# Reordered first loads, one chunk's statistics on ScalarE, and moved filler products in an attention and gated-MLP kernel

## The chip, the cores and the metric

The kernel runs on one core of one Trainium2 chip. The metric is device time in microseconds (us). Nine runs of the kernel before the change have a median of 799.55 us (799.35 to 801.16).

## The reference

Two residual blocks follow each other on x of shape 2048 x 1024, in bf16.

```python
h  = x + A(layernorm(x), wq, wk, wv, wo, beta)
h2 = h + B(layernorm(h), w_in, w_sp, b_sp, w_out)
```

A is attention with 32 heads of width 32 over four segments of 512 rows. Within a segment it is causal softmax attention. Beside it each head keeps a memory M and a sum z of earlier segments: with phi(t) = t + 1 for t > 0 and exp(t) otherwise, the memory's output is phi(q) M / (phi(q) z + 1e-6), and after each segment M gains phi(k)^T v and z gains the sum of phi(k). Both outputs are mixed by the gate sigmoid(beta) of the head, and the result is multiplied by wo.

B is a gated MLP: z = gelu(x w_in) with 3584 columns is split in halves z1 and z2, z2 is layer-normalized and mixed along the sequence by the 2048 x 2048 matrix w_sp, plus a bias b_sp for each row; the product with z1 goes through w_out.

## The kernel before, in words

The whole program is a list of operations. Each call of `G.op` (L93) records an operation with its engine, a cost in ns and the tiles that it reads and writes, from which its dependences follow. `schedule` (L150) then plays the list through a model of five engines: TensorE (PE) keeps the order in which its operations were recorded; ScalarE (ACT), VectorE (DVE), GpSimd (POOL) and SyncE (SP) take whatever is ready, by the place in the list plus a priority. The model's costs, with its model of DMA time (L211 to L215), thus fix the order on these four engines once and for all; on the chip each engine runs its own order and waits on semaphores (`link`, L232; `run`, L318). SP issues all DMAs, and at the end waits for the last count of every DMA semaphore (L1041, `dma_ends` of L304).

The start (L507 to L786). PE runs 14 warm-up products on zeros (`N_WARM`). SP loads x chunk by chunk (128 rows each; chunk 0 in two halves of its columns), wv, wq and wk by halves of their columns (`w_half`), and beta. `layernorm` (L524) of a chunk is two `bn_stats` of 512 columns and a `bn_aggr` on VectorE, the addition of epsilon (`pts1`) and the power -0.5 (`ptt`) on GpSimd, and the scaling (`ts`) in place on VectorE. `x_turn_pe` (L567) turns a chunk with 8 transposes on PE, four to a bank of PSUM; the first four are copied to XNT by VectorE, the others by ScalarE. Of the products with wv's first half, 8 to a chunk, the turn of the next chunk is put ahead of number 5 (`AT`). Then come the first q and k products and beta's gate.

The attention (L789 to L883) goes through 32 groups n of four heads (segment s = n // 8, c = n % 8) in 16 pairs. A pair has five logit rounds. In each, PE makes logits in four banks (`logits`, 4 or 8 products with 32 rows), ScalarE takes the exponential of all 2048 columns into E, and GpSimd masks it; the next round's logits need those banks again. Between the rounds stand other products in an order written out by hand: the projections `Pq` and `Pk`, the products with V (`X`, `MZU`, which ends in `combine` on VectorE and a transposing DMA into OT), and five slots of filler products. A filler is a V group (`v_group`: 8 products of 512 columns, copied by ScalarE) of a later or the same segment, or a wo group (`wo_group`: 8 products, an addition on VectorE, and at its second half the output's store, the layernorm of h and a transposing DMA). `plan` lays out which fillers go to which n, `order` to which slots: (2, 4, 0, 4, 1) in pairs 0 to 14, with two fillers in pairs 0 to 3, 12 and 14 and four in the others. In segment 0, `Pq` of n > 0 is copied by VectorE, otherwise by ScalarE. `chores` records the loads and layernorms of later chunks, and the second halves of wq, wk and wo.

The gated MLP (L886 to L1015) follows with products of 512 columns, gelu on ScalarE and additions and multiplications on VectorE. The change doesn't touch it.

Of the kernel before, what the change touches and what calls it, by code (L numbers as in the profile page):

```python
# [10 lines left out]
ACTF = mybir.ActivationFunctionType  # L11
# [24 lines left out]
class _Prog:  # L36
# [113 lines left out]
    def schedule(self):  # L150
        ops = self.ops
        n = len(ops)
        for o in ops:
            o.users = []
            o.ndep = len(o.deps)
            o.t0 = o.t1 = None
        for o in ops:
            for d in o.deps:
                ops[d].users.append(o.idx)
        pe_seq = [o.idx for o in ops if o.eng == PE]  # L160
        pe_at = 0
# [12 lines left out]

        while done < n:
            best = None
            if pe_at < len(pe_seq):
                o = ops[pe_seq[pe_at]]
                if o.ndep == 0:
                    best = (max(free[PE], rt[o.idx]), 0, PE, o.idx)  # L180
            for e in (ACT, DVE, POOL, SP):
                r, a = ready[e], avail[e]
                while r and r[0][0] <= free[e]:
                    _, p, i = heapq.heappop(r)
                    heapq.heappush(a, (p, i))
# [24 lines left out]
            free[e] = start + cost  # L210
            if o.dma:  # L211
                b = max(start + 2000.0, dma_free)
                dma_free = b + o.nbytes / 370.0
                o.t1 = dma_free + 50.0
                free[e] = start + cost  # L215
            else:
                o.t1 = start + cost + o.lag
            order[e].append(i)
            done += 1
            for u in o.users:  # L220
                w = ops[u]
                w.ndep -= 1
                t = o.t1 + (lag_same if w.eng == e and not o.dma else lag_x)
                if t > rt[u]:
                    rt[u] = t
                if w.ndep == 0 and w.eng != PE:
                    heapq.heappush(ready[w.eng], (rt[u], w.prio, u))
        self.order = order
        return max(o.t1 for o in ops)


    def link(self):  # L232
# [66 lines left out]
        for i in self.order[SP] + self.order[POOL] + self.order[ACT]:  # L299
            o = ops[i]  # L300
            if o.dma:
                cnt[o.sem] += 16
                o.semval = cnt[o.sem]
        self.dma_ends = [(dsem[j], cnt[j]) for j in range(npool)]  # L304
        for o in ops:
            w = []
            for q, v in o.waits.items():
# [22 lines left out]
def bass_sequential_preLN__memory_aug_infini_attn__mixer_gmlp__prompt_kernel(  # L330
# [87 lines left out]

    N_WARM = 14
    AT = [5, 5, 5, 9]  # L420
    BYACT = [0, 0, 0, 0]
    PS = nc.alloc_psum_tensor("ps", [128, 8, 512], F32)
    G.psum = PS.name

# [9 lines left out]
    def mm(o, lhsT, rhs, start, stop):  # L434
        n = n_of(rhs)
        G.op(PE, lambda e: e.matmul(o, lhsT, rhs, start=start, stop=stop), [lhsT, rhs], [o],  # L436
             max(n / 2.4 + 2.6, 25.0), lag=166, name="mm " + lhsT.tensor.name + " " + rhs.tensor.name)
# [50 lines left out]
    def pset(o, v):  # L488
        G.op(POOL, lambda e: e.memset(o, v), [], [o], (150 + n_of(o)) / 1.2, name="memset")

    def dma(o, i, transpose=False, after=False):
        nb = n_of(o) * list(o.ap)[0][1] * mybir.dt.size(o.dtype)
        d = G.op(SP, lambda e: e.dma_start(o, i, transpose=transpose), [i], [o], 1230.0 if transpose else 400.0, dma=True,  # L493
             nbytes=nb * (2.1 if transpose else 1.0), name=("T:" if transpose else "D:") + o.tensor.name)
        if after:
            d.deps.add(G.last_pe)
# [11 lines left out]
    G.op(DVE, lambda e: e.memset(ZERO[:], 0.0), [], [ZERO[:]], 200, name="memset")  # L508
    for k in range(N_WARM):
        mm(PS[:, 7, :], ZERO[:, 0:128], ZERO[:], True, True)  # L510
    for h in range(2):
        dma(XIN[0][:, h * 512:(h + 1) * 512], x2d[0:128, h * 512:(h + 1) * 512])
    iot = tens("iot", [128, 128], I32, R_E)
    G.op(POOL, lambda e: e.iota(iot[:], [[1, 128]], base=0, channel_multiplier=-1), [], [iot[:]], 400)
    pset(MHALF[:], -0.5)
# [5 lines left out]

    ln_rr = [0]

    def layernorm(src, dst, w, prio=0, by_act=False):  # L524
        late[0] = prio
        k = ln_rr[0] % 4
        ln_rr[0] += 1
        nch = (w + 511) // 512
        cs = w // nch
        for ci in range(nch):  # L530
            si, so = src[:, ci * cs:(ci + 1) * cs], STATS[k][:, ci, :]
            G.op(DVE, lambda e, si=si, so=so: e.bn_stats(so, si), [si], [so], (cs + 143) / 0.96, name="bn_stats",  # L532
                 prio=late[0])
        sa, mv = STATS[k][:, 0:nch, :], MV[k][:, 0:2]
        G.op(DVE, lambda e: e.bn_aggr(mv, sa), [sa], [mv], 250, name="bn_aggr", prio=late[0])  # L535
        pts1(RS[k][:], MV[k][:, 1:2], LN_EPS, ALU.add)
        ptt(RS[k][:], RS[k][:], MHALF[:], ALU.pow)
        if by_act:
            nm, mean, rs = MV[k][:, 2:3], MV[k][:, 0:1], RS[k][:]
            G.op(POOL, lambda e: e.scalar_tensor_tensor(nm, mean, -1.0, rs, ALU.mult, ALU.mult), [mean, rs], [nm],  # L540
                 220, name="nmr")
            act(dst, src, ACTF.Identity, scale=rs, bias=nm)
        else:
            ts(dst, src, MV[k][:, 0:1], RS[k][:], ALU.subtract, ALU.mult)
        late[0] = 0


    NJ = [512, 384, 256, 128]
# [13 lines left out]
    def x_load(tc):  # L562
        dma(XIN[tc % 4][:], x2d[tc * 128:(tc + 1) * 128, :])
# [4 lines left out]
    def x_turn_pe(tc):  # L568
        dst = XNT[0][:, :, tc * 128:(tc + 1) * 128]
        for h in range(2):  # L570
            bb = bank().bitcast(BF16)
            for i in range(4):
                c = 4 * h + i
                tr(bb[:, i * 128:(i + 1) * 128], XIN[tc][:, c * 128:(c + 1) * 128])
            bv = bb[:, 0:512].rearrange("p (c n) -> p c n", c=4)
            if h == 0:
                late[0] = -200
                copy(dst[:, 0:4, :], bv)
                late[0] = 0
            else:  # L580
                act(dst[:, 4:8, :], bv, ACTF.Copy)

    def x_turn(tc):
        s, tcl = divmod(tc, 4)
# [158 lines left out]
            dma(HNT[s][:, :, tcl * 128:(tcl + 1) * 128], hx[:], transpose=True)  # L743


    x_load(1)
    w_half(WV, A_wv, 0)
    x_load(2)
    x_load(3)
    w_half(WQ, A_wq, 0)  # L750
    w_half(WK, A_wk, 0)
# [2 lines left out]
    for i in range(2):  # L754
        pset(V[i][:, :, :, 32:34], 1.0)
    bank_rr[0] = 0
    for tcl in range(4):
        layernorm(XIN[tcl][:], XIN[tcl][:], D, by_act=BYACT[tcl])
    x_turn_pe(0)
    for tcl in range(4):  # L760
        b = bank()
# [25 lines left out]


    bank_set[0] = [4, 5, 6, 7]  # L789
    plan = []  # L790
    for n in range(32):
        s, c = divmod(n, 8)
        vs, wos = [], []
        if s == 0:
            vs = [(0, c, 1)] if c < 4 else [(1, c - 4, 0)]
        elif s <= 2:
            vs = [(s, 2 * c, 1), (s, 2 * c + 1, 1)] if c < 2 else [(s + 1, c - 4, 0)] if c >= 4 else []
        elif c < 4:
            vs = [(3, c, 1)]
        if 1 <= s <= 3:  # L800
            k = (0, 0, 2, 2, 1, 1, 1, 1) if s <= 2 else (0, 0, 1, 1, 1, 1, 2, 2)
            wos = [(s - 1, g) for g in range(sum(k[:c]), sum(k[:c + 1]))]
        plan.append((vs, wos))
    WINB = []
    for k, (c0, w) in enumerate(((1792, 512), (2304, 512), (2816, 512), (3328, 256), (0, 512), (512, 512),
                                 (1024, 512), (1536, 256))):
# [33 lines left out]

    for pair in range(16):
        a, b = 2 * pair, 2 * pair + 1
        fill = [(v_group, x) for n in (a, b) for x in plan[n][0]] + [(wo_group, x) for n in (a, b) for x in plan[n][1]]
        for n in (b + 1, b + 2):
            if n < 32:
                for x in plan[n][1]:
                    if x[1] % 2 == 0:
                        h_load(4 * x[0] + x[1] // 2)
        slots = [[] for _ in range(5)]
        order = (2, 4, 0, 4, 1) if pair < 15 else (2, 2, 3, 4)  # L850
        for k, x in enumerate(fill):
            slots[order[k]].append(x)

# [217 lines left out]
```

## Time and profile before

| | |
|---|---|
| median of 9 runs | 799.55 us |
| the profiled execution's own time | 800.15 us |
| its span in the trace | 798.4 us |
| PE, VectorE, ScalarE, GpSimd busy | 791.7, 369.8, 293.0, 140.2 us |
| first transpose of x on PE | 7.54 us |
| first q product | 18.58 us |
| first logits of pair 0, of pair 1 | 22.15, 36.82 us |
| last logits of the attention | 294.15 us |
| last addition on VectorE | 795.69 us |

Lines of the profile read thus. In a timeline: start, length, engine, line, operation, tiles (out<-in), shape, count, and in brackets how long the engine stood idle ahead of it and for whom. In a list of waits: who waited for whom, the total in us, how often, the longest. In a table of stretches: the stretch and its length, then busy us and number of instructions for PE, PE's weight loads, VectorE, ScalarE and GpSimd, the granted clock, the share of the DMA engines and GB/s. The line of an operation is often that of a helper: L436 is `mm`, L441 the logits, L445 the transposes, L450 `act`, L466 the scaling, L532 `bn_stats`, L493 every DMA, L1042 the final waits.

### The profile page before, as it was taken

What the parts mean: (1) busy time and instruction counts of PE and PEld (TensorE: products, weight loads), DVE (VectorE), ACT (ScalarE), POOL (GpSimd) and SP (SyncE); (2) the same over time, 40 slices, a digit from 0 to 9 for tenths busy, and PEclk for the clock granted to TensorE, in tenths of its full rate; (3) what the DMA queues carried; (4) which work ended last, traced back from release to release, by engine and by line L of the source; (5) the groups of instructions that cost most, each with busy time, mean ns of one, the idle gap of its engine ahead of it and who ended that gap; (6) DMA issues with size and microseconds to landing.
All of it is one profiled execution on the core that took longest, in us unless ns stands there. A gap on an engine that the chain in (4) does not pass through costs nothing.

```text
span 798.4 us, 12667 instructions
## 1 busy us (share of the span) xinstructions
PE 791.7 (99%) x5380; PEld 382.0 (48%) x5380; DVE 369.8 (46%) x849; ACT 293.0 (37%) x329; POOL 140.2 (18%) x273
## 2 busy tenths in 40 slices
PE   8999999999999999999999999999999999999998
PEld 3455555555554555445445454444444444444444
DVE  5883578968875586704224051133223223322332
ACT  2888867776788872133333333100000000000000
POOL 2464434443443341100001010000000000000000
PEclk9999999999999999999999999999999999999999
DMA  9757514452433548520000026803400620021001
GB/s 298 157 140 162 130 41 99 94 101 69 77 71 89 171 90 227 169 46 1 0 1 1 16 54 133 200 1 71 120 27 1 137 81 1 0 60 53 1 7 47
DMA packets 128457, 64.80 MB, mean 81 GB/s; under 512 B 95504, under 2 KB 120336, under 8 KB 128400
## 3 DMA queue, kind: packets, MB, share of 16 engines
q1 hardware_dynamic: 128400, 63.99, 33.2%
q8 instruction: 42, 0.69, 0.4%
q14 instruction: 15, 0.12, 0.1%
HBM read 32.51 MB, written 8.39 MB: 51 GB/s over the span
## 4 chain that ended last, share of the span: by engine, by line
PE 97%; DMA 1%; ACT 1%; DVE 1%; SPq 0%; issue 0%
PE ps L436 94%; PE ps L441 3%; DMA xin<-in_A_x_dram 1%; ACT e L450 0%; DVE stats L532 0%; SPq L493 0%; PE ps L445 0%; ACT qk L450 0%; DVE xin L466 0%; ACT ex L450 0%; DVE xnT L462 0%; DVE hx L472 0%; DVE mv L535 0%
## 5 line engine op out<-in xcount | busy, mean ns | idle before, releaser
L436 PE MATMUL ps<-wspT,z 128*128 128x512 bf16 x896 | 194.0, 379 | 0.0
L450 ACT ACTIVATE e<-ps 128x2048 bf16<-128x2048 f32 x80 | 149.7, 1872 | 40.0 <-PE ps L441 40.0
L436 PEld LDWEIGHTS ps<-wspT,z 128*128 128x128 bf16 x896 | 87.5, 98 | 105.8
L450 ACT ACTIVATE z<-ps 128x512 bf16<-128x512 f32 x120 | 68.2, 568 | 140.2 <-PE ps L436 140.2
L472 DVE TENSOR_TENSOR tg<-ps,brow 128x512 bf16<-128x512 f32 x56 | 38.7, 691 | 152.7 <-PE ps L436 122.5
L436 PE MATMUL ps<-win,hnT 128*128 128x512 bf16 (+1 forms) x512 | 97.8, 353 | 0.0
L436 PE MATMUL ps<-wout,y 128*128 128x512 bf16 (+2 forms) x462 | 97.4, 373 | 0.0
L436 PE MATMUL ps<-hnT,win 128*128 128x512 bf16 x448 | 97.3, 379 | 0.0
L653 POOL TENSOR_SCALAR_AFFINE_SELECT e<-e 128x1024 bf16<-128x1024 bf16 (+1 forms) x80 | 75.7, 946 | 107.0 <-ACT e L450 106.6
L532 DVE BATCH_NORM_STATS2 stats<-z 128x6 f32<-128x448 bf16 x64 | 39.9, 623 | 94.1 <-ACT z L450 92.6
L472 DVE TENSOR_TENSOR hx<-hx,ps 128x512 bf16<-128x512 bf16 (+1 forms) x65 | 43.7, 678 | 84.6 <-PE ps L436 82.3
L436 PEld LDWEIGHTS ps<-win,hnT 128*128 128x128 bf16 x512 | 50.0, 98 | 47.9
L436 PEld LDWEIGHTS ps<-wout,y 128*128 128x128 bf16 x462 | 44.6, 98 | 52.4
L436 PEld LDWEIGHTS ps<-hnT,win 128*128 128x128 bf16 x448 | 43.8, 98 | 52.3
L436 PE MATMUL ps<-wv,xnT 128*128 128x512 bf16 x256 | 60.2, 379 | 0.9 <-DMA wv<-in_A_wv_dram 0.9
L436 PE MATMUL ps<-xnT,wk 128*128 128x512 bf16 (+2 forms) x264 | 60.8, 374 | 0.0
L436 PE MATMUL ps<-xnT,wq 128*128 128x512 bf16 x256 | 60.8, 381 | 0.0
L436 PE MATMUL ps<-wo,oT 128*128 128x512 bf16 x256 | 59.0, 379 | 0.0
L486 POOL TENSOR_SCALAR rs<-mv 128x1 f32<-128x1 f32 x48 | 11.1, 230 | 193.1 <-DVE mv L535 191.7
L436 PEld LDWEIGHTS ps<-v,e 128*128 128x128 bf16 x1280 | 40.1, 96 | 9.1 <-issue 0.9
L436 PE MATMUL ps<-v,e 128*128 128x33 bf16 x1280 | 42.1, 178 | 0.0
L436 PEld LDWEIGHTS ps<-wo,oT 128*128 128x128 bf16 x256 | 24.7, 98 | 28.5 <-DVE ta L472 0.2
(58 smaller groups left out, 573.1 us busy)
## 6 DMA issues: line engine op xcount, KB each, us to landing
win<-in_B_w_in_dram SPq DMA_DIRECT2D x6, 1024.0 KB, 6.1
hx<-in_A_x_dram SPq DMA_DIRECT2D x16, 256.0 KB, 2.9
out_dram<-hx SPq DMA_DIRECT2D x16, 256.0 KB, 2.4
hx<-out_dram SPq DMA_DIRECT2D x16, 256.0 KB, 2.7
out_dram<-hx SPq DMA_DIRECT2D x31, 128.0 KB, 1.8
xin<-in_A_x_dram SPq DMA_DIRECT2D x15, 256.0 KB, 3.9
wout<-in_B_w_out_dram SPq DMA_DIRECT2D x2, 1792.0 KB, 10.0
wv<-in_A_wv_dram SPq DMA_DIRECT2D x2, 1024.0 KB, 9.6
```

Of the source, the lines that this page charges most:

```text
L436: G.op(PE, lambda e: e.matmul(o, lhsT, rhs, start=start, stop=stop), [lhsT, rhs], [o], max(n / 2.4 + 2.6, 25.0), lag=166, name="mm " + lhs ...
L441: G.op(PE, lambda e: e.matmul(o, lhsT, rhs, start=True, stop=True, tile_position=(32 * i, 0)), [lhsT, rhs], [o], n / 2.4 if last else 3.5, ...
L450: G.op(ACT, lambda e: e.activation(o, i, func, scale=scale, **kw), r, [o], ((172 if inps(i) else 224) + n_of(i)) / 1.2 + 26, prio=prio, na ...
L472: G.op(DVE, lambda e: e.tensor_tensor(o, a, b, op), [a, b], [o], vcost(o, [a, b], fast), name="tt", prio=late[0])
L486: G.op(POOL, lambda e: e.tensor_single_scalar(o, i, s, op), [i], [o], 220 if n_of(o) < 8 else 220 + 2.5 * n_of(o), name="pts1", prio=late[0])
L532: G.op(DVE, lambda e, si=si, so=so: e.bn_stats(so, si), [si], [so], (cs + 143) / 0.96, name="bn_stats", prio=late[0])
L653: G.op(POOL, lambda e: e.affine_select(d, d, pat, ALU.is_ge, 0.0, base=0, channel_multiplier=-1), [d], [d], 1270 if j else 640, name="mask")
```

## The change

Six edits go together. The planner's model of DMA time gets other constants, with 700 ns for transfers of 200,000 bytes or more, and the planned cost of `bn_aggr` goes from 250 to 210. The final waits are sorted by the planned end of each semaphore's last transfer. The first loads are recorded in the order x0 (two halves), x1, x2, wv in three pieces of its rows, x3, wq, wk. Chunk 1's mean and sum of squares come from two ScalarE passes with accumulator outputs (`layernorm_act`); for the other three chunks epsilon is added on VectorE, and the second `bn_stats` of a chunk is recorded as depending on the scaling of the chunk before it that VectorE treats. The copies of the turned chunks are assigned by the table `TCOPY`: both to VectorE for chunk 0. And the fillers of each pair, their slots and the engine that copies a V group are written out in `FILL`: pair 0 has four V groups instead of two, pair 4 two instead of four, and the pairs behind it have between two and five.

```diff
             if o.dma:
-                b = max(start + 2000.0, dma_free)
-                dma_free = b + o.nbytes / 370.0
-                o.t1 = dma_free + 50.0
+                b = max(start + 1850.0, dma_free)
+                dma_free = b + o.nbytes / 350.0
+                o.t1 = dma_free + (700.0 if o.nbytes >= 200000 else 50.0)
...
-        self.dma_ends = [(dsem[j], cnt[j]) for j in range(npool)]
+        ends = {}
+        for o in ops:
+            if o.dma and o.semval == cnt[o.sem]:
+                ends[o.sem] = o.t1
+        self.dma_ends = [(dsem[j], cnt[j]) for j in sorted(range(npool), key=lambda j: ends[j])]
...
-    BYACT = [0, 0, 0, 0]
+    TCOPY = [(DVE, DVE), (DVE, ACT), (DVE, ACT), (DVE, ACT)]
...
+    def x_cols(tc, h):
+        dma(XIN[tc][:, h * 512:(h + 1) * 512], x2d[tc * 128:(tc + 1) * 128, h * 512:(h + 1) * 512])
+
+    def wv_rows(a, b):
+        dma(WV[:, a:b, 0:512], A_wv.rearrange("(c p) n -> p c n", p=128)[:, a:b, 0:512])
+
     for h in range(2):
-        dma(XIN[0][:, h * 512:(h + 1) * 512], x2d[0:128, h * 512:(h + 1) * 512])
+        x_cols(0, h)
+    for tc in (1, 2):
+        dma(XIN[tc][:], x2d[tc * 128:(tc + 1) * 128, :])
+    for a, b in ((0, 4), (4, 6), (6, 8)):
+        wv_rows(a, b)
+    act(G1[:, 0:1], ZERO[:, 0:1], ACTF.Identity)
...
-    def layernorm(src, dst, w, prio=0, by_act=False):
+    def layernorm(src, dst, w, prio=0, first=None):
...
+            if ci and first is not None:
+                o.deps.update(first)
         sa, mv = STATS[k][:, 0:nch, :], MV[k][:, 0:2]
-        G.op(DVE, lambda e: e.bn_aggr(mv, sa), [sa], [mv], 250, name="bn_aggr", prio=late[0])
-        pts1(RS[k][:], MV[k][:, 1:2], LN_EPS, ALU.add)
+        G.op(DVE, lambda e: e.bn_aggr(mv, sa), [sa], [mv], 210, name="bn_aggr", prio=late[0])
+        if first is not None:
+            ts1(RS[k][:], MV[k][:, 1:2], LN_EPS, ALU.add, fast=1)
+        else:
+            pts1(RS[k][:], MV[k][:, 1:2], LN_EPS, ALU.add)
...
+    def layernorm_act(src, dst, junk, k):
+        nm, ss = MV[k][:, 0:1], MV[k][:, 1:2]
+        G.op(ACT, lambda e: e.activation(junk, src, ACTF.Identity, scale=-1.0 / D, accum_out=nm), [src], [junk, nm],
+             1250, name="sum")
+        G.op(ACT, lambda e: e.activation(junk, src, ACTF.Square, bias=nm, accum_out=ss), [src, nm], [junk, ss],
+             1250, name="sumsq")
+        G.op(POOL, lambda e: e.tensor_scalar(RS[k][:], ss, 1.0 / D, LN_EPS, ALU.mult, ALU.add), [ss], [RS[k][:]],
+             220, name="pts")
+        ptt(RS[k][:], RS[k][:], MHALF[:], ALU.pow)
+        ts(dst, src, nm, RS[k][:], ALU.add, ALU.mult)
...
-            if h == 0:
+            if TCOPY[tc][h] == DVE:
                 late[0] = -200
-                copy(dst[:, 0:4, :], bv)
+                copy(dst[:, 4 * h:4 * h + 4, :], bv)
                 late[0] = 0
             else:
-                act(dst[:, 4:8, :], bv, ACTF.Copy)
+                act(dst[:, 4 * h:4 * h + 4, :], bv, ACTF.Copy)
...
-    x_load(1)
-    w_half(WV, A_wv, 0)
-    x_load(2)
     x_load(3)
     w_half(WQ, A_wq, 0)
...
+    norm = []
     for tcl in range(4):
-        layernorm(XIN[tcl][:], XIN[tcl][:], D, by_act=BYACT[tcl])
+        if tcl == 1:
+            layernorm_act(XIN[1][:], XIN[1][:], HX[0][:], 3)
+        else:
+            norm = [layernorm(XIN[tcl][:], XIN[tcl][:], D, first=norm)]
...
+    FILL = [
+        (vf((0, 0, 1)) + vf((0, 1, 1)) + vf((0, 2, 1)) + vf((0, 3, 1), eng=DVE), (0, 1, 2, 4,)),
+        (vf((1, 0, 0)) + vf((1, 0, 1), eng=DVE), (2, 4,)),
+        (vf((1, 1, 0)) + vf((1, 1, 1), eng=DVE), (2, 4,)),
+        (vf((1, 2, 0)) + vf((1, 3, 0), eng=DVE), (2, 4,)),
+        (vf((1, 2, 1)) + vf((1, 3, 1), eng=DVE), (2, 4,)),
+        (wf(0, 0, 1) + wf(0, 1, 2) + wf(0, 2, 3) + wf(0, 3, 4), (2, 4, 0, 4,)),
+        (vf((2, 0, 0)) + vf((2, 1, 0)) + wf(0, 4, 5), (2, 4, 1,)),
+        (wf(0, 5, 6) + vf((2, 2, 0)) + vf((2, 3, 0)) + wf(0, 6, 7) + wf(0, 7, 8), (0, 2, 4, 0, 4,)),
+        (vf((2, 0, 1)) + vf((2, 1, 1)) + vf((2, 2, 1)) + vf((2, 3, 1)), (2, 4, 0, 4,)),
+        (wf(1, 0, 1) + wf(1, 3, 4) + wf(1, 2, 3) + wf(1, 1, 2), (2, 4, 0, 4,)),
+        (vf((3, 0, 0)) + vf((3, 1, 0)) + wf(1, 4, 5) + wf(1, 5, 6), (2, 4, 0, 4,)),
+        (vf((3, 2, 0)) + vf((3, 3, 0)) + wf(1, 6, 7) + wf(1, 7, 8), (2, 4, 0, 4,)),
+        (vf((3, 0, 1)) + vf((3, 1, 1)) + wf(2, 0, 1), (2, 0, 4,)),
+        (vf((3, 2, 1)) + wf(2, 1, 2) + vf((3, 3, 1)), (1, 2, 4,)),
+        (wf(2, 2, 3) + wf(2, 3, 4), (2, 4,)),
+        (wf(2, 4, 5) + wf(2, 5, 6) + wf(2, 6, 7) + wf(2, 7, 8), (2, 2, 3, 4,)),
+    ]
...
     for pair in range(16):
         a, b = 2 * pair, 2 * pair + 1
-        fill = [(v_group, x) for n in (a, b) for x in plan[n][0]] + [(wo_group, x) for n in (a, b) for x in plan[n][1]]
-        for n in (b + 1, b + 2):
-            if n < 32:
-                for x in plan[n][1]:
-                    if x[1] % 2 == 0:
-                        h_load(4 * x[0] + x[1] // 2)
+        fill, order = FILL[pair]
+        for p in (pair + 1,) if pair < 15 else ():
+            for f, x in FILL[p][0]:
+                if f == wo_group and x[1] % 2 == 0:
+                    h_load(4 * x[0] + x[1] // 2)
         slots = [[] for _ in range(5)]
-        order = (2, 4, 0, 4, 1) if pair < 15 else (2, 2, 3, 4)
```

In `FILL`, a V group is (segment, chunk, half of the columns), a wo group (segment, number); `vf` and `wf` list them, and the tuple behind them gives each one's slot. The rest of the planner, of PE's order within a pair and of the MLP is unchanged.

More of the change, by code (lines that the diff above doesn't have):

```diff
@@ L489, in pset, with dma @@
         G.op(POOL, lambda e: e.memset(o, v), [], [o], (150 + n_of(o)) / 1.2, name="memset")
-    def dma(o, i, transpose=False, after=False):
+    def dma(o, i, transpose=False, after=False, eng=SP):
         nb = n_of(o) * list(o.ap)[0][1] * mybir.dt.size(o.dtype)
-        d = G.op(SP, lambda e: e.dma_start(o, i, transpose=transpose), [i], [o], 1230.0 if transpose else 400.0, dma=True,
+        d = G.op(eng, lambda e: e.dma_start(o, i, transpose=transpose), [i], [o], 1230.0 if transpose else 400.0, dma=True,
              nbytes=nb * (2.1 if transpose else 1.0), name=("T:" if transpose else "D:") + o.tensor.name)
@@ L531, in layernorm @@
             si, so = src[:, ci * cs:(ci + 1) * cs], STATS[k][:, ci, :]
-            G.op(DVE, lambda e, si=si, so=so: e.bn_stats(so, si), [si], [so], (cs + 143) / 0.96, name="bn_stats",
-                 prio=late[0])
+            o = G.op(DVE, lambda e, si=si, so=so: e.bn_stats(so, si), [si], [so], (cs + 143) / 0.96, name="bn_stats",
+                     prio=late[0])
+            if ci and first is not None:
+                o.deps.update(first)
         sa, mv = STATS[k][:, 0:nch, :], MV[k][:, 0:2]
-        G.op(DVE, lambda e: e.bn_aggr(mv, sa), [sa], [mv], 250, name="bn_aggr", prio=late[0])
-        pts1(RS[k][:], MV[k][:, 1:2], LN_EPS, ALU.add)
-        ptt(RS[k][:], RS[k][:], MHALF[:], ALU.pow)
[L538 to L544, printed above, removed]
-        late[0] = 0
+        G.op(DVE, lambda e: e.bn_aggr(mv, sa), [sa], [mv], 210, name="bn_aggr", prio=late[0])
[3 more added lines that the diff above has]
+            pts1(RS[k][:], MV[k][:, 1:2], LN_EPS, ALU.add)
+        ptt(RS[k][:], RS[k][:], MHALF[:], ALU.pow)
+        ts(dst, src, MV[k][:, 0:1], RS[k][:], ALU.subtract, ALU.mult)
+        late[0] = 0
+        return len(G.ops) - 1
+    def layernorm_act(src, dst, junk, k):
[8 more added lines that the diff above has]
+        ts(dst, src, nm, RS[k][:], ALU.add, ALU.mult)
     NJ = [512, 384, 256, 128]
@@ L789, in bass_sequential_preLN__memory_aug_infini_attn__mixer_gmlp__prompt_kernel, with vf, wf @@
     bank_set[0] = [4, 5, 6, 7]
[L790 to L803, printed above, removed]
+    def vf(*x, eng=ACT):
+        return [(v_group, y + (eng,)) for y in x]
+    def wf(sg, a, b):
+        return [(wo_group, (sg, g)) for g in range(a, b)]
+    FILL = [
[16 more added lines that the diff above has]
+    ]
     WINB = []
```

## The prediction

> **What bounds the kernel now.** I read the page first: busy shares, and the chain that ended last.
>
> ```profile
> PE 791.7 (99%) x5380; PEld 382.0 (48%) x5380; DVE 369.8 (46%) x849; ACT 293.0 (37%) x329; POOL 140.2 (18%) x273
> ...
> PE 97%; DMA 1%; ACT 1%; DVE 1%; SPq 0%; issue 0%
> ```
>
> TensorE is the bound. A busy PE may still be stalled, though, since matmuls overlap; so next come its waits, and busy time by stretches.
>
> ```profile
> PE ps L445 <- DVE xin L466: 1.3, 3, 0.5
> ...
> PE ps L436 <- DMA wv<-in_A_wv_dram: 0.9, 1, 0.9
> PE ps L441 <- ACT qk L450: 0.2, 1, 0.2
> PE ps L441 <- ACT e L450: 0.2, 1, 0.2
> ```
>
> ```profile
> 28.00:296.00 268.00, 268.00 (x2813) 137.69 (x2812) 192.03 (x517) 210.43 (x191) 114.52 (x207) 1.00 0.49 109
> ```
>
> The attention stretch has PE busy 268.00 of 268 us, and no wait listed there. To be sure I went through the starts of consecutive matmuls: from 27.7 us on, only two gaps are over 0.12 us above the streaming time, of 0.17 us each. So moving products between rounds can win only where PE stalls today, ahead of 28 us. PE's own timeline there (start, length with the tail of the last matmul):
>
> ```profile
> 7.54 0.62 PE L445 MATMUL ps<-ident,xin 128*128 128x128 bf16 x8 [0.30 <-DVE xin L466]
> 9.04 1.24 PE L436 MATMUL ps<-wv,xnT 128*128 128x512 bf16 x5 [0.88 <-DMA wv<-in_A_wv_dram]
> 10.80 0.62 PE L445 MATMUL ps<-ident,xin 128*128 128x128 bf16 x8 [0.53 <-DVE xin L466]
> 11.26 1.89 PE L436 MATMUL ps<-wv,xnT 128*128 128x512 bf16 x8
> 13.57 0.62 PE L445 MATMUL ps<-ident,xin 128*128 128x128 bf16 x8 [0.42 <-DVE xin L466]
> ...
> 18.58 1.89 PE L436 MATMUL ps<-xnT,wq 128*128 128x512 bf16 x8
> ...
> 22.48 1.90 PE L436 MATMUL ps<-xnT,wq 128*128 128x512 bf16 x8
> 24.57 0.40 PE L441 MATMUL ps<-qk 32*128 32x384 bf16 x8 [0.19 <-ACT e L450]
> 24.90 1.90 PE L436 MATMUL ps<-xnT,wk 128*128 128x512 bf16 x8
> 26.95 0.29 PE L441 MATMUL ps<-qk 32*128 32x256 bf16 x4
> 27.49 0.29 PE L441 MATMUL ps<-qk 32*128 32x256 bf16 x4 [0.25 <-ACT qk L450]
> ```
>
> Price of dense work, from starts: 8 products of 512 columns take 1.73 us (18.58 to the next group at 20.31), 0.2165 each; 8 transposes 0.45; a logits round 0.33. From 7.54 to 18.58 are 11.04 us, of which 4 x 0.45 + 32 x 0.2165 = 8.73 are work: **2.31 us of stall** (1.05 ahead of 9.04, 0.68 ahead of 10.80, 0.58 ahead of 13.57). In the first pair: 22.48 + 1.73 = 24.21, next start 24.57, so 0.36; 26.63 to 26.95, 0.32; 27.12 to 27.49, 0.37: **1.05 us**. VectorE's timeline says why the first stall exists:
>
> ```profile
> 5.61 1.42 DVE L532 BATCH_NORM_STATS2 stats<-xin 128x6 f32<-128x512 bf16 x2 [0.89 <-DMA xin<-in_A_x_dram]
> 6.95 0.53 DVE L466 TENSOR_SCALAR xin<-xin,mv,rs 128x1024 bf16<-128x1024 bf16 x1
> ...
> 9.60 0.69 DVE L532 BATCH_NORM_STATS2 stats<-xin 128x6 f32<-128x512 bf16 x1 [1.21 <-DMA xin<-in_A_x_dram]
> 10.21 0.53 DVE L466 TENSOR_SCALAR xin<-xin,mv,rs 128x1024 bf16<-128x1024 bf16 x1
> ```
>
> GpSimd has 1/sigma of chunk 0 at 5.69 and of chunk 1 at 8.56, but in-order VectorE stands in the statistics of the next chunk, which wait for their load; the scalings come 1.2 and 1.6 us late. And the end of SyncE's program:
>
> ```profile
> L1042 SPq EVENT_SEMAPHORE  x8: 17/28/28, 797.5 to 797.9; - x8
> ```
>
> The eight final waits stand after the last landing (797.50), 0.062 apart.
>
> **What the Trainium skill says.** "TensorE: Matmul & The Clock Gate", Back-to-back issue gap: a warm matmul starts N/2.4 + 2.5 ns after the one before; the trace's 0.2165 us at 512 agrees. "DMA: Bandwidth & Descriptors", Queues, rings and completion order: one engine's issues share a ring that is consumed in order; the trace agrees, chunks and wv land in the order issued. "ScalarE: Activation LUTs", What ACT_TABLE_LOAD costs: 186 ns + 0.833 ns an element, 93 ns more for a pointer operand; 1039 ns for 1024 elements, and the trace's 1024-element exp (ex) has 1053. Its section on table sets counts identity and copy among functions of every set; Square isn't named, and no run shows it.
>
> **The change, part by part** (profiled time 800.15 us: span 798.4 and 1.75 around it).
>
> *Queue order, chunk 1 on ScalarE, epsilon on VectorE.* Chunk 0's scaling can start at about 5.7 instead of 6.95, but PE's 14 warm-up products (0.427 apart from 1.24) last until 7.22: first transposes at 7.24, 0.30 earlier. Both copies are now VectorE's; the first ends 0.85 after the transposes start (7.54 to 8.39 today), at 8.09. Landings by bytes: wv's second piece ends with the same 1.57 MB moved as all of wv today (x0, x1, wv), so at 8.9; the first piece 0.26 MB earlier at some 380 GB/s, 8.2; the third at 9.6; x3 at 10.3, as now. So products start at 8.35 (today's landing to start is 0.14) instead of 9.04, and five last to 9.43.
>
> Chunk 1 lands as today, 5.6. Sum and sum of squares: 1039 and 1132 ns by the page, with an accumulator output that no row shows. Bounds: nothing, or 0.25 each; I take 0.15 each, 2.5 us in all, so 8.15. GpSimd 0.23 + 0.57 and three hand-overs of 0.08: 9.2. Scaling 0.53: transposes at 9.8 instead of 10.80, stall 0.37. From there I follow VectorE in its order: tile 1's copy 10.23 to 10.65, half of x3's statistics 11.3, chunk 2's scaling 11.85, the other half 12.55, tile 2's copy 12.95, aggregate and epsilon (0.2 + 0.15, nearest row rm<-ps 148 ns; it replaces a GpSimd row of 0.23 and a hand-over) 13.3, GpSimd's power 13.97, chunk 3's scaling 14.53. PE meanwhile: second transposes 9.8 to 10.25, products to 11.98, transposes and products to 14.16, stall 0.41 to 14.57; then 0.45 + 11 x 0.2165 = 2.83, Q at 17.4. Stalls 0.66 + 0.37 + 0.41 against 2.31, and 0.30 at the start: **-1.18**. Bounds: -1.85 if only wv binds; 0 if chunk 1 comes 1.2 late. The planner puts tile 1's copy and x3's statistics close together; the other order adds some 0.5. The extra DMA issues cost nothing: SyncE issues one in 0.47, eight by 4.6, and the ring is full until 20 us. Beta lands at 19.5 as before; ScalarE waits for it ahead of the first q copy, needed at 21.
>
> *Two more V products in pair 0.* Each round gets 1.73 us more PE work, more than each stall (0.32 to 0.37); ScalarE has 1.87 exp + 0.6 + 0.6 against 3.8 us of PE a round: **-1.05**. wv's second half must be there by 22.9; it lands at 19.3.
>
> *Two fewer in pair 4; redistribution later.* Products are conserved (28 V, 24 of wo). Pair 4 then has two products, like pair 12 of today, which runs 15.2 us without stall though ScalarE has 5 x 1.87 + 4 x 0.60 + 2 x 0.63 + 2 x 0.60 = 14.2. Pair 4: one V copy less, its two ex of 1.05 instead of 0.63: 14.45 of 15.4. Bounds 0 and 0.8; I take **+0.10**. Pair 12 takes its first wo product at its end: the head's oT is issued 2.1 us after its PE work and lands 2.4 to 4.5 later, 6.6 at most, and it is asked for 7.6 later. Nothing; up to 1 if SyncE is late. V copies moved to VectorE (0.68 each, one a pair in pairs 0 to 4): hidden by the next 5 us of PE work before that bank is reused. wk's second half lands 1.3 us ahead of use in pair 1, relative to which nothing moves.
>
> *Final waits sorted by end.* All but the last are consumed before it: 7 x 0.062 = **-0.44**. A new model of DMA time in the planner reorders other engines; off the path, nothing.
>
> Sum: -1.18 - 1.05 + 0.10 - 0.44 = **-2.57**; 800.15 gives 797.58. The median of the runs is 0.60 below the profiled one: **797.0**.
>
> **Rivals.**
> 1. *VectorE never late*, PE waits for wv alone: head -1.85, sum -3.24, **796.3**. For: 1/sigma is ready early. Against: chunk 3's chain is serial on VectorE.
> 2. *ScalarE's statistics late*: a table load for Square (1.28, the trace's load) or long accumulator reads hold chunk 1 until 11: head gain 0, sum about -1.3, **798.2**. For: the whole chain hangs on one landing at 5.6 with two full passes; against: ScalarE idles there for 6.12 us.
> 3. *VectorE backlog in pairs 0 to 3* (slower): in that segment it copies q, too, which gates logits, and is busy 12.5 of 15.0 us; with 0.68 more a pair, if each of eight q copies came 0.68 beyond its slack, +5.4 - 2.6: **802.4**. It decides from 4.2 / 8 = 0.52 each. Against: q is asked for 2.7 to 5.5 us after its product.
>
> **Chances.** Forecast 0.63 (own range 796.4 to 797.9), rival 1 0.15, rival 2 0.15, rival 3 0.07. About 0.2%, 1.6 us, is what a measurement can tell from no change. Forecast and rival 1 are faster by more, 0.78; rival 2 within, 0.15; rival 3 slower, 0.07. The range runs from below rival 1 (pair 4 free, 0.3 more at the head) to above rival 2: 795.9 to 798.6.
>
> **What would show it.** First wv products near 8.35, second transposes near 9.8, Q near 17.4; no PE wait in pair 0; pair 4 about 15.4 us long; one final wait after the last landing. Wrong if PE has waits after 28 us, a second early table load, or Q not before 18.4.

## The result, and the profile after

| | before | after |
|---|---|---|
| median | 799.77 us (29 runs) | 796.81 us (9 runs: 796.31 to 797.71) |
| ratio | 1 | 0.9961, interval 0.9953 to 0.9970 |
| profiled execution | 800.15, span 798.4 | 796.57, span 794.8 |
| first transposes, Q products start | 7.54, 18.58 | 6.54, 16.52 |
| stall of PE from the first transposes to Q (8.73 of work taken off) | 2.31 | 1.25 |
| stall of PE in pair 0 | 1.05 | none over 0.1 |
| last DMA issue to the end of the span | 2.40 | 1.93 |

The kernel became 2.96 us faster by the medians, 3.1 by the ratio (0.0039 x 799.77); the forecast was 797.0. The two profiled executions differ by more, 3.58, and part of that is chance, which is taken apart below.

The page of the kernel after shows the same bound as before, a little tighter: busy shares, then the chain that ended last.

```profile
PE 790.3 (99%) x5380; PEld 381.5 (48%) x5380; DVE 370.6 (47%) x855; ACT 292.6 (37%) x328; POOL 141.5 (18%) x270
...
PE 98%; DMA 1%; DVE 0%; SPq 0%; issue 0%; POOL 0%
```

All that PE waits for in the kernel after (us in total, times, longest), to be held against the list of before:

```profile
PE ps L440 <- DVE zero L512: 1.2, 1, 1.2
PE ps L440 <- DMA wv<-in_A_wv_dram: 0.7, 1, 0.7
PE ps L449 <- DVE xin L470: 0.2, 1, 0.2
```

The first is the start of the program, as before. Three late chunks have become one of 0.2 us, and the two waits of the logits (ACT qk, ACT e) are gone. PE's timeline of the kernel after says where:

```profile
6.54 0.61 PE L449 MATMUL ps<-ident,xin 128*128 128x128 bf16 x8
7.89 1.24 PE L440 MATMUL ps<-wv,xnT 128*128 128x512 bf16 x5 [0.75 <-DMA wv<-in_A_wv_dram]
8.97 0.61 PE L449 MATMUL ps<-ident,xin 128*128 128x128 bf16 x8
...
13.69 0.62 PE L449 MATMUL ps<-ident,xin 128*128 128x128 bf16 x8 [0.21 <-DVE xin L470]
...
16.52 1.89 PE L440 MATMUL ps<-xnT,wq 128*128 128x512 bf16 x8
...
20.42 1.90 PE L440 MATMUL ps<-xnT,wq 128*128 128x512 bf16 x8
22.16 1.89 PE L440 MATMUL ps<-wv,xnT 128*128 128x512 bf16 x8
23.98 0.40 PE L445 MATMUL ps<-qk 32*128 32x384 bf16 x8
```

The second transposes follow five products without a stall (7.89 + 5 x 0.2165 = 8.97). In the whole head, counted from start to start, PE loses 0.90 ahead of the first wv products and 0.37 ahead of the fourth transposes. In pair 0 the eight V products now stand where the logits used to wait: 22.16 is 1.74 after 20.42, which is streaming time, and the logits start 0.09 beyond it. ScalarE's timeline in the kernel after shows the new statistics of chunk 1:

```profile
4.57 1.06 ACT L564 ACTIVATE hx<-xin 128x1024 bf16<-128x1024 bf16 x1 [2.29 <-DMA xin<-in_A_x_dram]
5.53 0.19 ACT L564 ACTIVATION_READ_ACCUMULATOR hx<-xin 128x1 f32 x1
5.75 1.15 ACT L566 ACTIVATE hx<-xin,mv 128x1024 bf16<-128x1024 bf16 x1
6.80 0.19 ACT L566 ACTIVATION_READ_ACCUMULATOR hx<-xin,mv 128x1 f32 x1
```

The accumulator comes out in an instruction of its own, 0.19 us, and no table is loaded between the two passes. From 4.57 to 6.99 they take 2.42 us; 2.5 had been counted. And the eight final waits of SyncE in the kernel after:

```profile
L1078 SPq EVENT_SEMAPHORE  x8: 17/28/28, 793.2 to 794.4; - x8
```

They are spread from 793.2 to 794.4 now. The last DMA is issued at 792.9 and lands 1.5 us later, at 794.4, so only one wait is left after the last landing.

### The profile page after: what moved, and what is told of

Read it like the earlier page. It is cut to its first block, busy times and chain, and to the rows that moved or that the text cites. A ratio compares the mean times of both kernels' runs of the same rounds, so it can differ in the third digit from the quotient of the medians.

```text
span 794.8 us, 12675 instructions
## 1 busy us (share of the span) xinstructions
PE 790.3 (99%) x5380; PEld 381.5 (48%) x5380; DVE 370.6 (47%) x855; ACT 292.6 (37%) x328; POOL 141.5 (18%) x270
## 4 chain that ended last, share of the span: by engine, by line
PE 98%; DMA 1%; DVE 0%; SPq 0%; issue 0%; POOL 0%
PE ps L440 95%; PE ps L445 3%; DMA xin<-in_A_x_dram 1%; SPq L497 0%; DVE stats L547 0%; DVE xin L470 0%; PE ps L449 0%; POOL rs L486 0%; DVE xnT L466 0%; DVE hx L476 0%; DVE rs L473 0%; DVE mv L552 0%
## 5 line engine op out<-in xcount | busy, mean ns | idle before, releaser
L679 POOL TENSOR_SCALAR_AFFINE_SELECT e<-e 128x1024 bf16<-128x1024 bf16 (+1 forms) x80 | 77.3, 966 | 121.7 <-ACT e L454 121.5
```

Source lines behind the costliest of these rows:

```text
L679: G.op(POOL, lambda e: e.affine_select(d, d, pat, ALU.is_ge, 0.0, base=0, channel_multiplier=-1), [d], [d], 1270 if j else 640, name="mask")
```

## The experiments

Twelve kernels, in three batches; each batch shares its runs of the kernel before (medians 799.48, 799.73, 799.49). An interval is 0.5 to 1 us wide to either side, so a difference of half a microsecond between two variants is read from the trace, not from the times.

**The three parts alone.** `tail_only` and `fill_only` are the kernel before with one part of the change; `head_only` is the kernel after without those two.

```diff
# tail_only
-        self.dma_ends = [(dsem[j], cnt[j]) for j in range(npool)]
...
+        self.dma_ends = [(dsem[j], cnt[j]) for j in sorted(range(npool), key=lambda j: ends[j])]
# fill_only
-        fill = [(v_group, x) for n in (a, b) for x in plan[n][0]] + [(wo_group, x) for n in (a, b) for x in plan[n][1]]
+        fill, order = FILL[pair]
...
# head_only: these two parts of after put back to those of before
```

> The kernel before with the sorted final waits alone. Theory (each edit removes its own stall, and the parts add up): 0.44 us less than the kernel before, about 799.3 against 799.77, with one final wait after the last landing instead of eight. Rival (the end is set by the landing itself, and what follows is fixed): no change.

> The kernel before with the written-out fillers alone (old loads, statistics, planner model, final waits). Theory: the three PE gaps of pair 0 vanish and none comes in pair 4, about 1.05 us less, 798.7. Rival (pair 4, with two products fewer, waits for the exponentials): gaps after 80 us, and 0 to 0.8 us of the gain given back. Q starts at about 18.6 as in the kernel before.

> The changed kernel with the old fillers and unsorted final waits: load order, chunk 1 on ScalarE, epsilon on VectorE, copies and planner model remain. Theory: Q starts at 16.5 to 17.2 us, and pair 0 keeps its three gaps; about 1.5 us less than before, 798.3 (2.96 measured in all, less 1.05 and 0.44). Rival (the earlier Q only makes pair 0 wait longer for beta or for wv's second half): pair 0's gaps grow beyond 1.1 us and less than 1 us is won.

| | median | ratio | change | forecast step |
|---|---|---|---|---|
| tail_only | 799.11 | 0.9992 (0.9984 to 1.0000) | -0.37 | -0.44 |
| fill_only | 798.50 | 0.9985 (0.9978 to 0.9991) | -0.98 | -1.05 and +0.10 |
| head_only | 798.45 | 0.9985 (0.9978 to 0.9993) | -1.03 | -1.18 |

The product of the ratios is 0.9962, the whole change 0.9961: within the intervals the parts add. In fill_only no gap is left in pair 0, and PE's list of waits has none over 0.2 us later on (its trace has 5284 of 5380 matmul records, and each missing one shows as a false gap of one product, 0.2 us). In head_only the three gaps of pair 0 stand as before: 0.35, 0.32 and 0.37.

A closer measure than the medians is the time of a profiled execution less its start of Q, since the scatter of the first loads lies ahead of Q. It is 781.57 us in before and 781.55 in head_only, 781.13 in tail_only, 780.49 in fill_only, 780.05 in after, and 780.02 to 780.06 in the eight variants below that keep its fillers and final waits. So the fillers are worth 1.08 us and the final waits 0.44, and they add to the 1.52 between before and after. What is left of a median is the head's part: 2.96 - 1.52 = 1.44 us in the runs of after, 1.01 in those of head_only.

PE's timeline of head_only is the fairest look at the head, as chunk 1 landed at 5.67 in it, near the 5.61 of the profile of before:

```profile
7.08 0.61 PE L445 MATMUL ps<-ident,xin 128*128 128x128 bf16 x8
8.49 1.24 PE L436 MATMUL ps<-wv,xnT 128*128 128x512 bf16 x5 [0.80 <-DMA wv<-in_A_wv_dram]
9.65 0.62 PE L445 MATMUL ps<-ident,xin 128*128 128x128 bf16 x8
...
14.29 0.62 PE L445 MATMUL ps<-ident,xin 128*128 128x128 bf16 x8
```

Its Q products start at 17.12, 1.46 ahead of the profile of before, while the medians give 1.03. The reason is that one profile of before isn't its mean: tail_only, whose head is that of before, has Q at 17.57 (chunk 1 landed at 5.00), and fill_only at 18.36 (5.71).

**The planner's constants.** `old_model` is the kernel after with the old cost of a DMA in the planner. PE and ScalarE keep their order of work. Up to the start of Q only VectorE's changes; later the order of some of SyncE's and GpSimd's work does, too, and the time behind Q (780.04) shows no effect of it.

```diff
-                b = max(start + 1850.0, dma_free)
-                dma_free = b + o.nbytes / 350.0
-                o.t1 = dma_free + (700.0 if o.nbytes >= 200000 else 50.0)
+                b = max(start + 2000.0, dma_free)
+                dma_free = b + o.nbytes / 370.0
+                o.t1 = dma_free + 50.0
```

> The changed kernel with the planner's old constants for DMA time. It computes the same, and only the orders on the engines differ: VectorE then has the first half of chunk 2's statistics ahead of chunk 0's scaling, and the first half of chunk 3's ahead of the copy of tile 1. Theory: that copy stands behind chunk 3's landing at 9.9 and ends near 11.0 instead of 9.8; Q about 0.6 us later than in the changed kernel, 797.4. Rival (VectorE's order there is hidden by the products): no difference, 796.8.

797.28, ratio 0.9967 (0.9955 to 0.9979): 2.2 us faster than before by the medians, 2.6 by the ratio, so some 0.5 to 0.8 of the gain is gone, though the intervals overlap. The trace shows what the order does. VectorE in old_model:

```profile
6.12 0.69 DVE L547 BATCH_NORM_STATS2 stats<-xin 128x6 f32<-128x512 bf16 x1 [1.17 <-DMA xin<-in_A_x_dram]
6.73 0.53 DVE L470 TENSOR_SCALAR xin<-xin,mv,rs 128x1024 bf16<-128x1024 bf16 x1
...
10.28 0.69 DVE L547 BATCH_NORM_STATS2 stats<-xin 128x6 f32<-128x512 bf16 x1 [0.64 <-DMA xin<-in_A_x_dram]
10.89 0.41 DVE L466 COPY xnT<-ps 128x512 bf16<-128x512 bf16 x1
```

GpSimd has 1/sigma of chunk 0 at 5.59, but the first half of chunk 2's statistics stands ahead of its scaling and waits for its load. This is the stall of the kernel before, made again by the order alone: the scaling comes 1.1 us late, and the first transposes start at 7.32, after PE has idled 1.55. Then chunk 3's statistics stand ahead of the copy of tile 1 and wait, too; PE's next products come 0.80 late, at 11.36. In the kernel after, that copy is at 9.39 and those statistics at 9.93.

**The order of the loads.** `x2_behind_wv` puts chunk 2 behind wv's pieces, `wv4_before_x2` between them; `wv_whole` and `wv_quarters` load wv's first half in one and in four pieces.

```diff
# x2_behind_wv
-    for tc in (1, 2):
-        dma(XIN[tc][:], x2d[tc * 128:(tc + 1) * 128, :])
+    dma(XIN[1][:], x2d[1 * 128:(1 + 1) * 128, :])
     for a, b in ((0, 4), (4, 6), (6, 8)):
         wv_rows(a, b)
+    dma(XIN[2][:], x2d[2 * 128:(2 + 1) * 128, :])
# wv_whole; wv_quarters has ((0, 2), (2, 4), (4, 6), (6, 8))
-    for a, b in ((0, 4), (4, 6), (6, 8)):
+    for a, b in ((0, 8),):
# wv4_before_x2: x1, wv rows 0 to 3, x2, wv rows 4 and 5, wv rows 6 and 7
```

> The changed kernel with x2 loaded behind wv's three pieces instead of ahead of them. Theory (VectorE's serial chain for chunks 2 and 3 sets the start of Q): wv's first piece comes 0.7 earlier, but x2 at about 9.5, and VectorE has its first half of statistics ahead of tile 1's copy; third transposes about 13.0 instead of 11.1 to 11.8, Q some 1.0 later, 797.8. Rival (wv's landing alone binds): products start 0.7 earlier and Q comes 0.5 earlier, 796.3.

> The changed kernel with wv's first piece loaded ahead of x2. Theory: products start 0.7 earlier, but the planner's order on VectorE changes: both halves of chunk 2's statistics ahead of chunk 1's scaling, and half of chunk 3's, which lands at 9.9, ahead of tile 1's copy; a gap of about 0.7 appears behind the second transposes, Q 0.3 to 0.6 later, 797.2. Rival (wv's landing binds): Q 0.5 earlier, 796.3.

> The changed kernel with wv's first half in four pieces of two row blocks; the orders on the engines stay the same. Theory: the first product can start when 0.26 MB less has moved, 0.6 earlier (7.4 to 7.9), but the second transposes wait for chunk 1's scaling (8.8 to 9.6), so the gap moves there and 0 to 0.3 is won: 796.6. Rival (wv's landing is what binds all through): Q 0.6 earlier, 796.2.

> The changed kernel with wv's first half in one load instead of three pieces. Theory: the first product waits for all of it, 1.3 us longer (about 9.1 to 9.7 instead of 7.9 to 8.5), and PE runs dense from there: Q 0.9 later, 797.7. Rival (VectorE's chain to chunk 3 hides it): Q within 0.3, 797.0.

x2_behind_wv took 798.19, ratio 0.9980 (0.9974 to 0.9987): -1.54. That is what the fillers and the final waits are worth (1.52), so by the times nothing of the head's gain is left. The first products are early (7.08), and then PE waits for scaled chunks three times, the third time 0.22; PE's timeline has the first two, and VectorE's what they waited for:

```profile
9.33 0.62 PE L449 MATMUL ps<-ident,xin 128*128 128x128 bf16 x8 [1.00 <-DVE xin L470]
...
12.50 0.62 PE L449 MATMUL ps<-ident,xin 128*128 128x128 bf16 x8 [0.82 <-DVE xin L470]
```

```profile
8.73 0.55 DVE L470 TENSOR_SCALAR xin<-xin,mv,rs 128x1024 bf16<-128x1024 bf16 x1 [1.38 <-POOL rs L486]
9.19 0.69 DVE L547 BATCH_NORM_STATS2 stats<-xin 128x6 f32<-128x512 bf16 x1
...
11.90 0.55 DVE L470 TENSOR_SCALAR xin<-xin,mv,rs 128x1024 bf16<-128x1024 bf16 x1
```

The first wait is not the stall of the kernel before: VectorE idles 1.38 us for chunk 1's 1/sigma, which comes from ScalarE and GpSimd, and the products ahead of it have only come earlier. The second is chunk 2's: its statistics begin at 9.19 instead of 6.07, and everything behind them is later. Whether its load or its place behind the scaling of chunk 1 sets that start, the trace doesn't say.

wv4_before_x2 took 797.16, ratio 0.9971 (0.9960 to 0.9983): its products start at 7.52, and the second transposes then wait 0.85 for chunk 1's scaling, which stands behind both halves of chunk 2's statistics. wv_quarters took 796.90, ratio 0.9970 (0.9959 to 0.9980), no different from after within the intervals: products start at 7.11 and stall 0.51 for the second piece.

With one piece the times change. The 22 runs of wv_whole lie in two groups, 13 from 796.81 to 798.00 and 9 from 800.07 to 801.71, with nothing between; the ratio over all, 0.9988 (0.9978 to 0.9998), describes neither. The profiled execution is of the upper group:

```profile
10.98 2.31 PE L440 MATMUL ps<-wv,xnT 128*128 128x512 bf16 x5 [3.90 <-DMA wv<-in_A_wv_dram]
13.09 1.06 PE L449 MATMUL ps<-ident,xin 128*128 128x128 bf16 x8
```

PE idles 3.90 us for wv, which lands at 10.98 instead of the expected 9.1 to 9.7, and afterwards five products take 13.09 - 10.98 = 2.11 us, 0.42 each: half the rate of dense work. Q starts at 21.68. The table of stretches shows when the granted clock (third number from the end) fell in wv_whole:

```profile
8.00:9.00 1.00, 0.00 (x0) 0.00 (x0) 0.96 (x4) 0.00 (x0) 0.09 (x1) 1.00 0.86 274
9.00:10.00 1.00, 0.00 (x0) 0.00 (x0) 0.01 (x1) 0.00 (x0) 0.55 (x1) 0.58 1.03 357
10.00:11.00 1.00, 0.02 (x1) 0.02 (x2) 0.00 (x0) 0.00 (x0) 0.00 (x0) 0.50 1.08 386
...
15.00:16.00 1.00, 1.00 (x4) 0.30 (x2) 0.18 (x2) 0.53 (x1) 0.55 (x1) 0.51 1.10 349
16.00:17.00 1.00, 1.00 (x10) 0.61 (x9) 0.00 (x0) 0.07 (x1) 0.00 (x0) 1.00 1.09 344
```

A mean of 0.58 between 9 and 10 us means half clock from 9.16 on (0.16 x 1 + 0.84 x 0.5 = 0.58); read alike, it ends at 15.98. The clock is on record for every run: 1.0 in all 13 of the lower group, 0.996 or 0.998 in all nine of the upper. So the groups are those without and with a stretch of half speed. But half speed isn't the whole distance. From 10.98 to Q it cost 10.70 - 8.28 = 2.4 us (8.28 is the dense time of the 32 products and 24 transposes there), while the profiled execution is 4.5 above the lower group's median of 797.2. By an estimate from their times less 780.04, the lower runs started Q at 16.8 to 18.0; this one would have started it at 19.3 without the half clock. So its products, which waited for wv alone, started later than in any run of the lower group. Why wv comes late in some runs, and where the clock fell in those that weren't profiled, stays open. My expectations had the wait but not its size, and not the clock.

**Who does the statistics.** `chunk1_dve` gives chunk 1 back to VectorE, `chunks12_act` gives chunk 2 to ScalarE as well.

```diff
# chunk1_dve: the branch below is never taken
-        if tcl == 1:
+        if tcl == 9:
# chunks12_act
-        if tcl == 1:
-            layernorm_act(XIN[1][:], XIN[1][:], HX[0][:], 3)
+        if tcl in (1, 2):
+            layernorm_act(XIN[tcl][:], XIN[tcl][:], HX[tcl - 1][:], 1 + tcl)
```

> The changed kernel with chunk 1's statistics on VectorE again, by the same function as the other chunks. Theory: VectorE then carries four chunks in series and its order puts half of the next chunk's statistics ahead of each scaling; fourth transposes about 0.9 later, Q 0.9 later, 797.7. Rival (the order of loads made the whole gain): Q within 0.3, 797.0.

> The changed kernel with chunk 2's statistics on ScalarE, too, behind chunk 1's. ScalarE is idle there until the copies. Theory: chunk 2 is scaled about when PE asks for it (sums end at 9.4 to 10.6, scaling by 11 to 12), VectorE is free for chunk 3, and the last gap (0.3 to 0.4) ahead of the fourth transposes closes: 796.5. Rival: ScalarE's copies of tile 1 (its second half and its V) stand behind the sums, or chunk 2 comes late: Q 0.3 to 0.8 later, 797.3.

chunk1_dve took 797.48, ratio 0.9970 (0.9960 to 0.9981): -2.25. Its trace has stalls of 0.76, 0.39 and 0.38 ahead of the second, third and fourth transposes and Q at 17.69, though chunk 1 landed at 4.96. VectorE doesn't stand at a load here: chunk 1's aggregate waits behind the copies of chunk 0, which wait for PE, and starts at 8.06, though its statistics ended at 6.86. What is left of the head's gain can't be said closely: by the times it is 2.25 - 1.52 = 0.73, by the traces nothing, since tail_only with the whole head of before and a like landing (5.00) has Q at 17.57.

chunks12_act took 797.24, ratio 0.9966 (0.9955 to 0.9978): no better than after. The last stall is gone (fourth transposes at 13.86 without a wait), but the third transposes wait instead, to 11.68. VectorE's timeline says why:

```profile
9.76 1.41 DVE L547 BATCH_NORM_STATS2 stats<-xin 128x6 f32<-128x512 bf16 x2
11.09 0.53 DVE L470 TENSOR_SCALAR xin<-xin,mv,rs 128x1024 bf16<-128x1024 bf16 x1
```

ScalarE's sums end at 9.74, as expected, and GpSimd has chunk 2's 1/sigma at 10.65, but the scaling stands behind both halves of chunk 3's statistics until 11.09. My expectation of 796.5 counted when ScalarE is done and not what VectorE has ahead of the scaling.

**Fillers taken away from a pair.** `thin14` moves the two wo products of pair 14 to pair 15, to price what pair 4 escaped.

```diff
-        (wf(2, 2, 3) + wf(2, 3, 4), (2, 4,)),
-        (wf(2, 4, 5) + wf(2, 5, 6) + wf(2, 6, 7) + wf(2, 7, 8), (2, 2, 3, 4,)),
+        ([], ()),
+        (wf(2, 2, 3) + wf(2, 3, 4) + wf(2, 4, 5) + wf(2, 5, 6) + wf(2, 6, 7) + wf(2, 7, 8), (0, 0, 2, 2, 3, 4,)),
```

> The changed kernel with pair 14's two wo products moved to pair 15, so that pair 14 has none. Theory (a pair needs two fillers to cover five exponentials with what ScalarE does between them): pair 14 has 11.7 us of PE work and needs about 14 to 14.7 us, so PE stalls 2.5 to 3 us there, pair 15 is 3.46 us longer, 799.5. Rival (ScalarE has slack enough at any filling, since the exponentials alone need 9.4 us): no gap above 0.3, 796.8.

798.23, ratio 0.9985 (0.9978 to 0.9992): -1.26, so 1.7 us slower than after by the medians, and 1.45 by the time less the start of Q (781.49 against 780.04). Its trace, too, has 5284 matmul records; the only wait of PE over 0.3 us behind the start of the program is this:

```profile
PE ps L445 <- ACT e L454: 1.5, 2, 1.3
```

With no filler, pair 14 takes 13.15 us (263.11 to 276.26) for 11.7 of PE work, and the logits wait for exp. The mechanism is the expected one, the size half of it, and ScalarE's timeline says why: its work in this pair is 5 x 1.87 of exp, 4 x 0.60 of copies and 2 x 0.62 of ex, 13.0 us, which is the length of the pair. I had counted 14 to 14.7; the 14.2 worked out for pair 12 holds two copies of V groups (0.60 each), and pair 14, whose fillers were wo groups, has none.

**The warm-up.** `warm10` issues 10 products of zeros ahead of the first transposes instead of 14 (`N_WARM = 10`).

> The changed kernel with 10 warm-up products instead of 14. Theory: PE's first transposes then start when chunk 0 is scaled (6.2), but the products still wait for wv at 7.9 to 8.5, so nothing is won: 796.8, Q unchanged. Rival (the array isn't warm yet or cools down again): products of 0.427 instead of 0.2165 from 7.9 us on, and several us more.

Eight runs, again in two groups: 796.12, 796.16, 796.17, 796.53 and 798.36, 799.13, 799.26, 800.31; the ratio over all is 0.9978 (0.9964 to 0.9992). The granted clock is 1.0 in the four lower runs and 0.996 or 0.998 in the four upper ones. The profiled execution (799.13) is of the upper group; PE's timeline, and the stretches in which its clock fell and rose again:

```profile
6.08 0.62 PE L449 MATMUL ps<-ident,xin 128*128 128x128 bf16 x8 [0.40 <-DVE xin L470]
8.92 1.87 PE L440 MATMUL ps<-wv,xnT 128*128 128x512 bf16 x5 [2.21 <-DVE xin L470]
10.58 1.06 PE L449 MATMUL ps<-ident,xin 128*128 128x128 bf16 x8
```

```profile
9.00:10.00 1.00, 1.00 (x4) 0.37 (x4) 0.13 (x1) 0.00 (x0) 0.55 (x1) 0.69 1.06 386
...
12.00:13.00 1.00, 1.00 (x5) 0.33 (x4) 0.96 (x3) 0.32 (x2) 0.00 (x0) 0.60 1.10 348
```

The bracket names chunk 1's scaling, but these products read wv and chunk 0; wv's first piece landed 6.1 us after its issue, at about 8.8, against 5.1 in the kernel after, and that is what they waited for. From the end of the first transposes PE idles some 2.4 us. The clock falls to half at 9.38, after the first products, and is back at 12.80. Half speed costs at most half of these 3.4 us, 1.7, of the 2.9 between this execution and the lower group; the products also start later, at 8.92 against 7.89 in the kernel after. So with less warm-up work PE idles longer ahead of wv, and part of the runs pay with half speed. The lower group wasn't profiled, so why it is 0.6 below after's median stays open.

## Why the prediction was right

**The head, -1.18.** Measured alone -1.03. By the time less the start of Q it is 1.44 in the runs of after, so the forecast lies between the two. Step by step, in the profile whose landing is like that of before (head_only): first wv products 8.49 (8.35 had been worked out), second transposes 9.65 (9.8), fourth 14.29 (14.57), Q 17.12 (17.4). The stalls were to be 0.66, 0.37 and 0.41; they are 0.96, 0.08 and 0.29, in all 1.33 instead of 1.44. The sizes moved between them: the first piece of wv binds more than worked out, chunk 1 less. The reading of the cause holds for the waits ahead of the first and second transposes: an in-order VectorE stood in statistics whose data hadn't landed, and old_model makes that stall again by its order alone. The largest stall of before, 1.05 ahead of the first wv products, is wv's own landing, which the lines of VectorE don't explain. Three profiles with the head of before (before, tail_only, fill_only) stall 2.31, 1.92 and 1.99 us between the first transposes and Q (8.73 of work taken off), three with that of after (after, head_only, thin14) 1.25, 1.31 and 1.02, so the gain doesn't hang on one landing. Without chunk 1 on ScalarE or with VectorE's old order the traces show stalls again (0.76 and 0.80), and without chunk 2 ahead of wv the head's gain is gone by the times as well. Epsilon on VectorE, the copies of chunk 0 and the dependence between chunks' statistics were not tried alone.

**What the profile of after shows beyond it.** Q at 16.52 is 0.9 earlier than worked out. Chunk 1 was there at 4.57 in that execution instead of 5.61, though SyncE's first issues stand at the same times, and the 14 warm-up products took 5.46 us instead of 5.99. Both vary from one execution to the next, whatever the kernel: over the profiles the first use of chunk 1 lies between 4.57 and 5.71, and 14 warm-up products took 4.54 to 6.15 us. So the profile of before had a late landing and that of after the earliest, and the pair differs by 3.58 where the medians differ by 2.96. One thing stays open here: with chunk 2 queued behind chunk 1, nine profiles have its first use at 4.57 to 5.67, mean 4.97; with wv behind it, five have 4.99 to 5.71, mean 5.33. The change may thus also bring chunk 1 in earlier, by some 0.4, which I had costed at nothing ("chunk 1 lands as today"); so few scattered values don't show it. Of the 3.58, 1.00 is the earlier start of the transposes, 1.06 fewer stalls in the head (2.31 - 1.25), 1.05 pair 0 and 0.47 the end; they sum to 3.58.

**Pair 0, -1.05; pair 4, +0.10.** fill_only measured -0.98 for both by the medians and -1.08 by the time less the start of Q, so pair 4 cost nothing. It shows no stall in the kernel after and takes 15.2 us (82.32 to 97.56; 15.4 had been worked out). Two products in a pair are enough, as pair 12 of before had suggested; thin14 shows that with none, ScalarE's work sets the length of the pair.

**The end, -0.44.** From the last DMA issue to the end of the span, 2.40 became 1.93: -0.47. tail_only measured -0.37 by the medians and -0.44 by the time less the start of Q.

**The moved wo product and the copies moved to VectorE, nothing.** No wait on either is in the list of after. **The rivals.** VectorE is still late once, by 0.37 (rival 1 had it never late); no second table load comes early and the accumulator reads took 0.19 each, within the bounds of 0 to 0.25 (rival 2); and PE's list of waits has none for a q copy (rival 3).

The sum came to -2.57 and the runs give -2.96 to -3.1; the three parts alone give -2.38. Behind the start of Q the account is close: 1.39 was forecast (1.05 - 0.10 + 0.44) and 1.52 measured. What the runs leave open is the head, 1.0 to 1.4; an earlier landing of chunk 1 would lie on the side of the remainder. That the forecast time misses the median by only 0.2 is in part luck: the step was 0.39 too small, and the base from which it was taken, 799.55, lies 0.22 below the later median of 799.77.

## What to carry to other kernels

Where an in-order engine does work for several loads, a late transfer holds back finished work behind it: order its instructions by when data really lands, and give one load's work to an engine that idles. Filler work pays only where TensorE stalls, and the donor must keep enough: two products a pair were enough to leave behind, and none cost 1.5 to 1.7 us. Ahead of a cut in warm-up work or a merge of first loads, ask how long TensorE will idle before its first real product.

## What the runs showed of the hardware

- TensorE's granted clock fell to half while PE idled for its first real products, or just behind that, in part of the runs of wv_whole and warm10. In the two profiles the half-speed stretches are 6.82 us (9.16 to 15.98) and 3.42 us (9.38 to 12.80) long. The groups of times lie 3.3 us (medians 797.2 and 800.6) and 3.0 us (796.2 and 799.2) apart; a later start of the products is part of that distance. One of the 21 runs of x2_behind_wv (799.85) has a clock of 0.998, too. The Trainium skill, "TensorE: Matmul & The Clock Gate", What's actually happening, says that the array falls back to half clock after at least one idle window of about 3.4 us, and that the window runs free of the program. The stretches agree with such a window once and twice. The condition doesn't: in wv_whole the clock fell 2.1 us after PE's last work (7.09), and in warm10 it fell after an idle of 2.4 us and 0.46 us of products; a window of 3.4 us that ends at the fall has work in it in both. Whether the phase of the window also decides which runs are hit isn't shown.
- The accumulator of an activation comes out in an instruction of its own of 0.19 us; a 1024-element pass with Square has 1.15 us and needed no table load after Identity.
- The same first load comes into use up to 1.1 us earlier or later from one profiled execution to another, also in one and the same queue order (chunk 1 behind chunk 0 and ahead of chunk 2: 4.57 in the kernel after, 5.67 in head_only). The cause was not tried.
